# The sigmoid-gated activation of a fused attention/MLP/MoE kernel: ScalarE's Sigmoid with VectorE's product, against ScalarE's Gelu_apprx_sigmoid evaluated twice from PSUM

## Chip, cores, metric

The kernel runs on one core of one Trainium2 chip, as one launch. The metric is the device time of that launch in microseconds, the median of several runs. Engines are named as in the profile: PE is TensorE (PEld its weight loads), DVE is VectorE, ACT is ScalarE, POOL is GpSimd, SP is SyncE, whose queue starts most DMAs.

## What is computed

Three stages on 4608 tokens of width 512: a linear attention, an MLP with a sigmoid-gated activation, and a mixture of eight experts. The change is in the activation `g` of the MLP:

```python
def _attn_ref(q, k, v):                 # 8 batches, 8 heads, 576 x 64
    q_s = softmax(q, axis=-1)           # over the head's width
    k_s = softmax(k, axis=2)            # over the sequence
    kv = np.einsum('bhsd,bhse->bhde', k_s, v)
    return np.einsum('bhsd,bhde->bhse', q_s, kv)

def _moe_ref(x, w_in, w_out):           # 512 -> 2048 -> 512
    h = x @ w_in
    g = h * (1.0 / (1.0 + np.exp(-1.702 * h)))
    return g @ w_out

def _moe2_ref(x, w_skip, w_gate, w1, w2):   # E = 8 experts, 512 -> 1024 -> 512
    # tokens with x @ w_skip > 0 go to the expert of the largest gate logit
    h = np.maximum(xc[mask] @ w1[e], 0.0)
    y[mask] = gate_w[mask, None] * (h @ w2[e])
    out[do_compute] = xc + y
```

The inputs are float32, the MLP's weights float64. Matmuls keep float32 accuracy by splitting each operand into an upper half (rounded to fp32r) and the rest (lower half): three fp32r matmuls, upper by upper, upper by lower and lower by upper, stand for one.

## The kernel before

The tokens are worked in nine chunks of 512 (`NCH`). For each chunk the MLP runs over 16 blocks m of 128 hidden units. `mm1(m)` (L441 to L443) makes the block's `h` in a PSUM bank `hps[m % 2]` out of 12 matmuls; `mm1_act(m)` turns it into `ghi[m % 3]` (upper half) and `glo[m % 3]` (lower half) in SBUF; `mm2(m)` (L470 to L472) multiplies these with `w_out` into four accumulators in 12 matmuls. The activation has four steps: `act_sig` (ACT, L446) writes sigmoid(1.702 h) into the one tile `sgt`; `act_mul` (DVE, L449) multiplies it with `h` out of the bank, in place; `act_hi` (ACT, L452) rounds `sgt` into `ghi`; `act_lo` (DVE, in the first and the last chunk POOL, L455) subtracts `ghi` from `sgt` into `glo`. The bank is free for block m+2 when `act_mul` has read it, and `sgt` is free for block m+1 when `act_lo` has read it.

Every engine works off its own instructions in the order in which the code issues them.

- **The start (chunk 0)** is issued in the order of the words of the string `START`: `sg`, `sm`, `gh` and `gl` with a block's number are the four steps above. Between them stand the attention of chunks 0 and 1 (`ka` is L269, DVE's maximum over K; `kb` L275 and `kt` L266 are PE transposes; `kv` L301 the product of K and V) and the splitting of the MLP's weights, piece by piece: `wl` loads 128 x 512 float64 (SP), `wa` takes the absolute value into one of two temporaries (ACT, L197), `wb` makes a float32 out of the bits in four steps on DVE (L209 to L212), `wh` rounds the upper half (ACT, L221), `wp` subtracts for the lower half (POOL, L225).
- **Chunks 1 to 8** run the loop over m: `mm1(m + 2)`, its `mm1_act`, `mm2(m)`, and then what the list `slots[m]` holds: attention for the next chunk, the gate's dot products of the chunk before (L487, DVE), and its routing. `route_b` (L569, L570) puts counts into a PSUM tile `att`, of which there are two; `route_c` (L577 to L592) is a chain of small DVE instructions that reads it. After m = 14 and 15 the next chunk's input is made by `x_prod` (L408, PE, into `att`) and split (L393 ACT, L420 DVE). `exp` of the attention and of the routing needs another ACT function table than the activation does, so an ACT_TABLE_LOAD stands at each switch.
- **The experts** follow the last chunk; there the activation is Relu (L973), which the change doesn't touch.

Of the kernel before, what the change touches and what calls it, by code (L numbers as in the profile page):

```python
# [40 lines left out]
START = """  # L41
kl.0.1 ql.0.0 ql.0.1 kl.0.0 kl.0.2 km.0.1 kl.0.3 kt.0.1 vl.0.1 ka.0.1 qm.0.0 kb.0.1 vl.0.3 ks.0.1
qs.0.0:G qm.0.1 ke.0.1 vl.0.0 km.0.0 qs.0.1:G qe.0.0 qr.0.0 wl.0.0.0 kt.0.0 vl.0.2 qe.0.1 km.0.2
qn.0.0:G kv.0.1 km.0.3 wl.5.1.1 qt.0.0.1 wl.1.0.2 ka.0.0 wl.0.2.3 qt.0.0.0 kb.0.0 qc.0.0.1:A qr.0.1
wl.0.1.6 qc.0.0.0:A wl.0.3.7 ks.0.0 wl.1.1.8 wl.4.1.9 wa.0.0.0 ke.0.0 kt.0.2 qn.0.1:G kr.0.1
wl.1.3.10 kn.0.1:V ka.0.2 wl.4.3.11 kt.0.3 kb.0.2 ka.0.3 qt.0.1.1 wl.4.0.12 ks.0.2 kb.0.3 qc.0.1.1:A
wl.1.2.13 ks.0.3 qt.0.1.0 ql.1.0 xm.0.1 ke.0.3 kv.0.0 wb.0.0 ct xh.0.1:A ke.0.2 cw wa.0.2.0 kr.0.0
vl.1.0 xl.0.1 kn.0.0:A kv.0.3 wb.0.2 qc.0.1.0:A kv.0.2 kl.1.1 wh.0.0 kr.0.3 vl.1.1 kr.0.2 wp.0.0:G
kn.0.3:A kn.0.2:V xm.0.3 wa.0.1.0 wb.0.1 ql.1.1 xm.0.2 xh.0.3:A wl.5.0.0 xl.0.3 xh.0.2:A kl.1.0
wh.0.1 xl.0.2 wa.4.1.0 wp.0.1:G xm.0.0 wl.4.2.5 xh.0.0:A wb.4.1 wl.5.2.4 wl.2.0.6 wh.0.2 wh.4.1  # L50
xl.0.0 m1.0 wp.0.2:G wa.1.1.0 wb.1.1 wl.2.1.3 m1.1 sg.0 wp.4.1:G sm.0 wa.4.0.0 wb.4.0 wh.1.1
wl.2.3.9 gh.0 gl.0:G m1.2 wa.0.3.1 wh.4.0 qm.1.0 wb.0.3 wa.1.0.0 sg.1 c2t c2c wp.4.0:G wh.0.3 c2d
sm.1 gh.1 m2.0 wb.1.0 wa.1.3.1 wl.5.3.12 wb.1.3 wa.1.2.0 wh.1.0 wb.1.2 wp.0.3:G gl.1:G wl.2.2.7 m1.3
sg.2 wh.1.3 wa.4.2.1 m2.1 wh.1.2 wb.4.2 wp.1.1:G wp.1.0:G wl.6.2.2 wa.5.0.0 wh.4.2 wp.1.3:G sm.2
wa.4.3.1 qm.1.1 gh.2 wp.1.2:G gl.2:G km.1.1 m1.4 km.1.0 wp.4.2:G sg.3 sm.3 wb.4.3 wl.3.0.5 m2.2 gh.3
wb.5.0 qs.1.0:G qe.1.0 m1.5 wa.2.1.1 wh.4.3 gl.3:G wh.5.0 qr.1.0 wa.2.0.0 kt.1.0 sg.4 wp.4.3:G
ka.1.0 sm.4 kt.1.1 kb.1.0 wp.5.0:G gh.4 m2.3 ka.1.1 gl.4:G m2.4 ks.1.0 wl.6.0.0 ke.1.0 wb.2.1 sg.5
kl.1.2 sm.5 wa.2.2.1 wb.2.2 qn.1.0:G gh.5 kb.1.1 m1.6 wh.2.1 wh.2.2 wb.2.0 qs.1.1:G wa.5.2.1 kv.1.0
m1.7 wb.5.2 gl.5:G wp.2.1:G wl.6.1.3 sg.6 vl.1.2 wh.2.0 wa.5.1.0 wb.5.1 wp.2.2:G wh.5.2 wa.2.3.1
wh.5.1 wb.2.3 wp.2.0:G wa.6.1.0 wp.5.1:G sm.6 qe.1.1 wa.5.3.1 kr.1.0 gh.6 wb.5.3 wl.7.2.1 wh.2.3  # L60
m2.5 kn.1.0:A wp.2.3:G wa.6.0.1 qr.1.1 wh.5.3 gl.6:G m1.8 km.1.2 wp.5.2:G sg.7 sm.7 wp.5.3:G m2.6
wl.3.1.4 gh.7 ks.1.1 wb.6.0 ke.1.1 kl.1.3 kt.1.2 m1.9 ka.1.2 gl.7:G wh.6.0 wa.3.0.1 wp.6.0:G sg.8
sm.8 m2.7 wl.3.2.0 wb.3.0 gh.8 gl.8:G m1.10 km.1.3 wa.3.1.1 wh.3.0 kt.1.3 wp.3.0:G sg.9 m2.8 sm.9
gh.9 wb.6.1 wl.3.3.5 wh.6.1 wb.3.1 wa.3.2.0 m1.11 wb.3.2 gl.9:G sg.10 wa.6.2.1 kb.1.2 wh.3.1 wb.6.2
wp.6.1:G wl.6.3.3 m2.9 wa.3.3.0 wh.3.2 wh.6.2 wb.3.3 wp.3.1:G wl.7.1.4 wa.6.3.1 sm.10 wp.3.2:G
wh.3.3 wa.7.2.0 wp.3.3:G ka.1.3 kb.1.3 wl.7.3.0 gh.10 gl.10:G ks.1.2 kv.1.1 ks.1.3 m1.12 wl.7.0.5
kr.1.1 ke.1.2 vl.1.3 wb.6.3 kn.1.1:A sg.11 kv.1.2 wh.6.3 wp.6.2:G qt.1.0.0 sm.11 gh.11 wa.7.0.1
m1.13 kr.1.2 wb.7.2 ke.1.3 wh.7.2 wb.7.0 wa.7.1.0 m2.10 kn.1.2:A kv.1.3 wb.7.1 wp.6.3:G gl.11:G
sg.12 wh.7.0 m2.11 wa.7.3.1 wp.7.0:G sm.12 wh.7.1 gh.12 wp.7.1:G kr.1.3 kn.1.3:V m1.14 gl.12:G
qc.1.0.0:A m2.12 wb.7.3 sg.13 sm.13 wp.7.2:G qt.1.0.1 gh.13 gl.13:G m1.15 qc.1.0.1:A qn.1.1:V  # L70
qt.1.1.0 wh.7.3 sg.14 qt.1.1.1 wp.7.3:G sm.14 qc.1.1.0:A m2.13 qc.1.1.1:V c2b gh.14 gl.14:G sg.15
xm.1.3 m2.14 sm.15 xh.1.3:A xl.1.3 gh.15 gl.15:G xm.1.1 m2.15 xh.1.1:A xl.1.1 xm.1.0 xm.1.2 xh.1.0:A
xl.1.0 xh.1.2:A xl.1.2
"""
# [1247 lines left out]
```

## Time and profile before

| | us |
|---|---|
| median of 3 runs | 1301.46 |
| lowest and highest | 1297.41, 1302.84 |
| the profiled execution, its own time | 1297.15 |
| its span, first to last instruction | 1295.4 |
| chunk 0 (the start) in it | 0 to 186.7 |
| chunks 1 to 8 | 186.7 to 982.7 |
| experts | 982.7 to 1295.4 |

A row of the profile names line, engine, operation and tiles (out<-in). "Idle" is time in which the engine of the row had nothing to do, and behind the arrow stands the instruction that ended it. The granted clock of PE is given as a share of full speed, with 0.974 in the mean over the span. In the timeline a row has the start and the duration; instructions of one engine overlap by about 0.1 us, so the distance between two starts is shorter than the duration.

### The profile page before, as it was taken

What the parts mean: (1) busy time and instruction counts of PE and PEld (TensorE: products, weight loads), DVE (VectorE), ACT (ScalarE), POOL (GpSimd) and SP (SyncE); (2) the same over time, 40 slices, a digit from 0 to 9 for tenths busy, and PEclk for the clock granted to TensorE, in tenths of its full rate; (3) what the DMA queues carried; (4) which work ended last, traced back from release to release, by engine and by line L of the source; (5) the groups of instructions that cost most, each with busy time, mean ns of one, the idle gap of its engine ahead of it and who ended that gap; (6) DMA issues with size and microseconds to landing.
All of it is one profiled execution on the core that took longest, in us unless ns stands there. A gap on an engine that the chain in (4) does not pass through costs nothing. (4 is left out here: it accounts for less than half of the span.)

```text
span 1295.4 us, 17224 instructions
## 1 busy us (share of the span) xinstructions
PE 1214.2 (94%) x6316; PEld 990.4 (76%) x6316; DVE 907.6 (70%) x1791; ACT 571.3 (44%) x774; POOL 204.0 (16%) x185
## 2 busy tenths in 40 slices
...
GB/s 288 238 52 74 91 168 67 47 25 92 50 6 114 48 11 107 46 19 99 47 27 98 37 1 98 1 1 66 27 234 99 169 280 209 256 215 233 222 168 142
DMA packets 109857, 138.25 MB, mean 107 GB/s; under 512 B 52805, under 2 KB 72517, under 8 KB 107314
## 3 DMA queue, kind: packets, MB, share of 16 engines
...
q14 instruction: 55, 0.45, 0.1%
...
## 5 line engine op out<-in xcount | busy, mean ns | idle before, releaser
L441 PE MATMUL hps<-xth,wh 128*128 128x512 f32 x576 | 238.4, 414 | 10.6 <-ACT wh L221 8.9
L470 PE MATMUL acc<-wh,ghi 128*128 128x512 f32 x576 | 232.2, 403 | 9.2 <-ACT wh L221 9.2
L442 PE MATMUL hps<-xtl,wh 128*128 128x512 f32 x576 | 229.9, 399 | 0.9 <-DVE xtl L420 0.9
L443 PE MATMUL hps<-xth,wl 128*128 128x512 f32 x576 | 229.9, 399 | 0.7 <-POOL wl L225 0.7
L471 PE MATMUL acc<-wl,ghi 128*128 128x512 f32 x576 | 227.8, 396 | 1.6 <-POOL wl L225 1.6
L472 PE MATMUL acc<-wh,glo 128*128 128x512 f32 x576 | 228.1, 396 | 0.5 <-POOL glo L455 0.5
L449 DVE TENSOR_TENSOR sgt<-hps,sgt 128x512 f32<-128x512 f32 x144 | 99.4, 690 | 157.6 <-ACT sgt L446 156.9
L446 ACT ACTIVATE sgt<-hps 128x512 f32<-128x512 f32 x144 | 86.2, 598 | 200.3 <-PE hps L443 174.5
L487 DVE CUSTOM_DVE_ANT_0 qb<-qx,wgb 128x512 f32<-128x512 f32 x225 | 160.6, 714 | 3.2
...
L452 ACT CAST ghi<-sgt 128x512 fp32r<-128x512 f32 x144 | 89.3, 620 | 127.8 <-DVE sgt L449 125.5
L441 PEld LDWEIGHTS hps<-xth,wh 128*128 128x128 f32 x576 | 111.1, 193 | 39.7 <-ACT wh L221 9.8
L470 PEld LDWEIGHTS acc<-wh,ghi 128*128 128x128 f32 x576 | 109.2, 190 | 35.0 <-ACT wh L221 9.6
L443 PEld LDWEIGHTS hps<-xth,wl 128*128 128x128 f32 x576 | 109.9, 191 | 27.6 <-POOL wl L225 1.1
L471 PEld LDWEIGHTS acc<-wl,ghi 128*128 128x128 f32 x576 | 109.1, 189 | 28.2 <-POOL wl L225 2.7
L442 PEld LDWEIGHTS hps<-xtl,wh 128*128 128x128 f32 x576 | 110.4, 192 | 24.5 <-DVE xtl L420 1.7
L472 PEld LDWEIGHTS acc<-wh,glo 128*128 128x128 f32 x576 | 109.2, 190 | 25.9 <-POOL glo L455 1.0
L966 PE MATMUL hps<-ghi,wh 128*128 128x256 f32 x352 | 100.3, 285 | 0.1
L968 PE MATMUL hps<-ghi,wl 128*128 128x256 f32 x352 | 99.1, 281 | 0.0
L967 PE MATMUL hps<-glo,wh 128*128 128x256 f32 x352 | 99.0, 281 | 0.0
L455 DVE TENSOR_TENSOR glo<-sgt,ghi 128x512 fp32r<-128x512 f32 x112 | 77.6, 693 | 26.0 <-ACT ghi L452 19.3
L983 PE MATMUL acc<-wh,xth 128*128 128x512 f32 x192 | 77.0, 401 | 0.0
...
## 6 DMA issues: line engine op xcount, KB each, us to landing
...
```

The costliest lines, as they stand in the source:

```text
L441: nc.tensor.matmul(hp, lhsT=wh[s][:, kk, cs], rhs=xth[:, kk], start=(kk == 0), stop=False)
L442: nc.tensor.matmul(hp, lhsT=wh[s][:, kk, cs], rhs=xtl[:, kk], start=False, stop=False)
L443: nc.tensor.matmul(hp, lhsT=wl[s][:, kk, cs], rhs=xth[:, kk], start=False, stop=(kk == 3))
L449: nc.vector.tensor_mul(out=sgt, in0=hps[m % 2], in1=sgt)
L452: nc.scalar.copy(out=ghi[m % 3], in_=sgt)
L470: nc.tensor.matmul(acc[r], lhsT=gh[:, cs], rhs=wh[4 + s][:, mm], start=(m == 0), stop=False)
L471: nc.tensor.matmul(acc[r], lhsT=gh[:, cs], rhs=wl[4 + s][:, mm], start=False, stop=False)
L472: nc.tensor.matmul(acc[r], lhsT=gl[:, cs], rhs=wh[4 + s][:, mm], start=False, stop=(m == 15))
L487: nc.vector.tensor_tensor_reduce(out=out, in0=qx[:, r, :], in1=wgb[:, e, :], scale=1.0, scalar=0.0, op0=ALU.mult, op1=ALU.add, accum_out=l ...
L966: nc.tensor.matmul(o, lhsT=wh[w][:, kk, cs], rhs=xh, start=(kk == 0), stop=False)
L967: nc.tensor.matmul(o, lhsT=wh[w][:, kk, cs], rhs=xl, start=False, stop=False)
L968: nc.tensor.matmul(o, lhsT=wl[w][:, kk, cs], rhs=xh, start=False, stop=(kk == 3))
```

## The change

`act_sig` and `act_mul` go. `act_hi` now evaluates `Gelu_apprx_sigmoid` on the PSUM bank and writes the rounded result straight into `ghi`; the new `act_all` evaluates the same function on the same bank once more and writes it unrounded into `sgt`. Both are on ACT. `act_lo` stays. In `START` the word `gh` moves to the place of `sg`, the new word `ga` (`act_all`) stands where `gh` stood, and `sm` is gone; all other words keep their order.

```diff
 START = """
...
-xl.0.0 m1.0 wp.0.2:G wa.1.1.0 wb.1.1 wl.2.1.3 m1.1 sg.0 wp.4.1:G sm.0 wa.4.0.0 wb.4.0 wh.1.1
-wl.2.3.9 gh.0 gl.0:G m1.2 wa.0.3.1 wh.4.0 qm.1.0 wb.0.3 wa.1.0.0 sg.1 c2t c2c wp.4.0:G wh.0.3 c2d
-sm.1 gh.1 m2.0 wb.1.0 wa.1.3.1 wl.5.3.12 wb.1.3 wa.1.2.0 wh.1.0 wb.1.2 wp.0.3:G gl.1:G wl.2.2.7 m1.3
+wb.1.1 wl.2.1.3 m1.1 gh.0 wp.4.1:G wa.4.0.0 wb.4.0 wh.1.1 wl.2.3.9 ga.0 gl.0:G m1.2 wa.0.3.1 wh.4.0
+qm.1.0 wb.0.3 wa.1.0.0 gh.1 c2t c2c wp.4.0:G wh.0.3 c2d ga.1 m2.0 wb.1.0 wa.1.3.1 wl.5.3.12 wb.1.3
...
-    def act_sig(m):
-        nc.scalar.activation(out=sgt, in_=hps[m % 2], func=AF.Sigmoid, scale=1.702)
-
-    def act_mul(m):
-        nc.vector.tensor_mul(out=sgt, in0=hps[m % 2], in1=sgt)
-
     def act_hi(m):
-        nc.scalar.copy(out=ghi[m % 3], in_=sgt)
+        nc.scalar.activation(out=ghi[m % 3], in_=hps[m % 2], func=AF.Gelu_apprx_sigmoid)
+
+    def act_all(m):
+        nc.scalar.activation(out=sgt, in_=hps[m % 2], func=AF.Gelu_apprx_sigmoid)
...
     def mm1_act(m, eng=nc.vector, fill=()):
-        act_sig(m)
-        act_mul(m)
         act_hi(m)
+        act_all(m)
         for f in fill:
             f()
         act_lo(m, eng)
...
-        "sg": act_sig,
-        "sm": act_mul,
         "gh": act_hi,
+        "ga": act_all,
         "gl": act_lo,
```

The instructions of each engine, as they stand in the two programs (line numbers of the later one are a few lower; the number behind a tile's name is its buffer):

DVE in the start, around block 8, before. L209 to L212 are a piece of weights, L269 and L256 maxima over K:

```order
L212 SCALAR_TENSOR_TENSOR wgb<-wgb 128x512
L269 TENSOR_REDUCE kmx<-att 128x1
L449 TENSOR_TENSOR sgt<-hps,sgt 128x512
L209 TENSOR_SCALAR wgb<-wgb 128x512
L210 TENSOR_SCALAR wgb<-wgb 128x512
L211 SCALAR_TENSOR_TENSOR wgb<-qx,wgb 128x512
L212 SCALAR_TENSOR_TENSOR qx<-qx,wgb 128x512
L256 TENSOR_REDUCE kpm_98<-kvr 128x128
L449 TENSOR_TENSOR sgt<-hps,sgt 128x512
L209 TENSOR_SCALAR kvr<-kvr 128x512
```

The same place after:

```order
L211 SCALAR_TENSOR_TENSOR wgb<-wgb 128x512
L268 TENSOR_REDUCE kmx<-att 128x1
L208 TENSOR_SCALAR wgb<-wgb 128x512
L209 TENSOR_SCALAR wgb<-wgb 128x512
L210 SCALAR_TENSOR_TENSOR wgb<-qx,wgb 128x512
L211 SCALAR_TENSOR_TENSOR qx<-qx,wgb 128x512
L255 TENSOR_REDUCE kpm_98<-kvr 128x128
L208 TENSOR_SCALAR kvr<-kvr 128x512
```

The two products are gone from between the pieces, and nothing else has moved.

DVE at the end of chunk 1, block 15 and the beginning of `route_c`, before:

```order
L550 TENSOR_TENSOR roh<-roh,rcm 128x32
L552 TENSOR_SCALAR rval<-misc 128x4
L449 TENSOR_TENSOR sgt<-hps,sgt 128x512
L455 TENSOR_TENSOR glo_89<-sgt,ghi_86 128x512
L577 COPY rrk<-att 128x32
```

After:

```order
L545 TENSOR_TENSOR roh<-roh,rcm 128x32
L547 TENSOR_SCALAR rval<-misc 128x4
L451 TENSOR_TENSOR glo_89<-sgt,ghi_86 128x512
L572 COPY rrk<-att 128x32
L574 TENSOR_TENSOR rrk<-rrk,misc 128x8
```

The subtraction is now the block's only instruction on DVE, ahead of `route_c`.

ACT at the same place, before:

```order
L558 ACT_TABLE_LOAD
L558 ACTIVATE rex<-rex 128x32
L446 ACT_TABLE_LOAD
L446 ACTIVATE sgt<-hps 128x512
L452 CAST ghi_86<-sgt 128x512
L393 COPY qx<-att 128x512
```

After:

```order
L553 ACT_TABLE_LOAD
L553 ACTIVATE rex<-rex 128x32
L445 ACT_TABLE_LOAD
L445 ACTIVATE ghi_86<-hps 128x512
L448 ACTIVATE sgt<-hps 128x512
L392 COPY qx<-att 128x512
```

ACT has as many instructions as before, in the same places, with as many table loads; the second of the block reads PSUM and no longer what DVE wrote.

## Rows read from the trace of the kernel before

**Rows 1.** Page, part 1: busy time and instructions of each engine.

```profile
PE 1214.2 (94%) x6316; PEld 990.4 (76%) x6316; DVE 907.6 (70%) x1791; ACT 571.3 (44%) x774; POOL 204.0 (16%) x185
```

**Rows 2.** Windows: stretch, length; busy (instructions) of PE, PEld, DVE, ACT, POOL; PE's clock, DMA.

```profile
46.00:146.30 100.30, 65.87 (x265) 49.31 (x263) 93.19 (x116) 52.00 (x78) 47.30 (x34) 0.85 0.34 113
146.30:186.70 40.40, 39.93 (x215) 31.09 (x215) 25.24 (x40) 23.14 (x37) 17.79 (x13) 0.91 0.36 105
389.00:488.00 99.00, 97.74 (x500) 78.39 (x498) 70.83 (x166) 44.50 (x65) 2.93 (x3) 1.00 0.21 56
```

**Rows 3.** Waits of PE in the start (total, times, longest), and PE's timeline at 146.

```profile
PE att L275 <- DVE kmx L269: 12.1, 3, 8.1
PE acc L470 <- ACT wh L221: 9.2, 1, 9.2
...
146.32 0.47 PE L275 MATMUL att<-ident,kmx 128*128 128x128 f32 x1 [8.07 <-DVE kmx L269]
```

**Rows 4.** Groups of DVE by form, 46 to 146.3: count, busy, mean ns, idle before.

```profile
L211 DVE SCALAR_TENSOR_TENSOR wgb<-qx,wgb 128x512 uint32<-128x512 uint32 x4 | 7.1, 1775 | 0.1
L449 DVE TENSOR_TENSOR sgt<-hps,sgt 128x512 f32<-128x512 f32 x10 | 6.8, 684 | 4.3 <-ACT sgt L446 4.3
...
L212 DVE SCALAR_TENSOR_TENSOR qx<-qx,wgb 128x512 uint32<-128x512 uint32 x4 | 2.8, 693 | 0.2
```

**Rows 5.** Timeline of DVE in the start around blocks 5 and 8: start, duration.

```profile
89.53 0.70 DVE L212 SCALAR_TENSOR_TENSOR wgb<-wgb 128x512 uint32<-128x512 uint32 x1
90.14 0.68 DVE L449 TENSOR_TENSOR sgt<-hps,sgt 128x512 f32<-128x512 f32 x1
90.95 0.43 DVE L209 TENSOR_SCALAR wgb<-wgb 128x512 f32<-128x512 f32 x1
...
120.06 0.28 DVE L269 TENSOR_REDUCE kmx<-att 128x1 f32<-128x128 f32 x1
123.35 0.69 DVE L449 TENSOR_TENSOR sgt<-hps,sgt 128x512 f32<-128x512 f32 x1 [3.00 <-ACT sgt L446]
123.95 0.42 DVE L209 TENSOR_SCALAR wgb<-wgb 128x512 f32<-128x512 f32 x1
```

**Rows 6.** Timeline of ACT at the same two places.

```profile
90.26 0.67 ACT L197 ACTIVATE wgb<-ewh 128x512 f32<-128x512 f32 x1 [2.88 <-DVE wgb L212]
...
120.74 0.67 ACT L197 ACTIVATE wgb<-qx 128x512 f32<-128x512 f32 x1
```

**Rows 7.** Groups of ACT by form, whole span: count, busy, mean ns, idle before.

```profile
L452 ACT CAST ghi<-sgt 128x512 fp32r<-128x512 f32 x144 | 89.3, 620 | 127.8 <-DVE sgt L449 125.5 <-DVE misc L915 2.3
L446 ACT ACTIVATE sgt<-hps 128x512 f32<-128x512 f32 x144 | 86.2, 598 | 200.3 <-PE hps L443 174.5 <-POOL glo L455 23.6 <-DVE glo L455 1.7
...
L973 ACT ACTIVATE xth<-hps 128x512 fp32r<-128x512 f32 x44 | 26.4, 600 | 104.6 <-issue 56.8 <-PE hps L968 40.3 <-ACT wh L928 7.6
```

**Rows 8.** Timelines of ACT, DVE and PE at the end of chunk 1.

```profile
275.24 0.60 ACT L446 ACTIVATE sgt<-hps 128x512 f32<-128x512 f32 x1
276.60 0.62 ACT L452 CAST ghi<-sgt 128x512 fp32r<-128x512 f32 x1 [0.76 <-DVE sgt L449]
...
277.25 0.69 DVE L455 TENSOR_TENSOR glo<-sgt,ghi 128x512 fp32r<-128x512 f32 x1 [0.68 <-ACT ghi L452]
277.86 0.19 DVE L577 COPY rrk<-att 128x32 f32<-128x32 f32 x1
...
277.01 0.39 PE L570 MATMUL att<-roh,ones 128*128 128x32 f32 x2
277.75 1.14 PE L408 MATMUL att<-qx,qb 128*128 128x128 f32 x4 [0.36 <-ACT qx L393]
279.77 0.46 PE L408 MATMUL att<-qx,qb 128*128 128x128 f32 x2 [0.88 <-DVE rrk L581]
```

**Rows 9.** Line 408 over the whole span: idle of PE before it, by releaser (us, times).

```profile
  DVE rrk L581: 6.2, 7
```

**Rows 10.** Timeline of PE at the end of the last chunk.

```profile
980.26 0.50 PE L472 MATMUL acc<-wh,glo 128*128 128x512 f32 x1 [0.52 <-POOL glo L455]
```

More of the change, by code (lines that the diff above doesn't have):

```diff
@@ L44 @@
 qn.0.0:G kv.0.1 km.0.3 wl.5.1.1 qt.0.0.1 wl.1.0.2 ka.0.0 wl.0.2.3 qt.0.0.0 kb.0.0 qc.0.0.1:A qr.0.1
[L45 to L49, printed above, removed]
@@ L50 @@
-wh.0.1 xl.0.2 wa.4.1.0 wp.0.1:G xm.0.0 wl.4.2.5 xh.0.0:A wb.4.1 wl.5.2.4 wl.2.0.6 wh.0.2 wh.4.1
-xl.0.0 m1.0 wp.0.2:G wa.1.1.0 wb.1.1 wl.2.1.3 m1.1 sg.0 wp.4.1:G sm.0 wa.4.0.0 wb.4.0 wh.1.1
-wl.2.3.9 gh.0 gl.0:G m1.2 wa.0.3.1 wh.4.0 qm.1.0 wb.0.3 wa.1.0.0 sg.1 c2t c2c wp.4.0:G wh.0.3 c2d
-sm.1 gh.1 m2.0 wb.1.0 wa.1.3.1 wl.5.3.12 wb.1.3 wa.1.2.0 wh.1.0 wb.1.2 wp.0.3:G gl.1:G wl.2.2.7 m1.3
-sg.2 wh.1.3 wa.4.2.1 m2.1 wh.1.2 wb.4.2 wp.1.1:G wp.1.0:G wl.6.2.2 wa.5.0.0 wh.4.2 wp.1.3:G sm.2
-wa.4.3.1 qm.1.1 gh.2 wp.1.2:G gl.2:G km.1.1 m1.4 km.1.0 wp.4.2:G sg.3 sm.3 wb.4.3 wl.3.0.5 m2.2 gh.3
@@ L56 @@
[L56 to L73, printed above, removed]
+wl.0.1.6 qc.0.0.0:A wl.0.3.7 ks.0.0 wl.1.1.8 wl.4.1.9 wa.0.0.0 ke.0.0 kt.0.2 qn.0.1:G kr.0.1 wl.1.3.10
@@ new lines @@
+kn.0.1:V ka.0.2 wl.4.3.11 kt.0.3 kb.0.2 ka.0.3 qt.0.1.1 wl.4.0.12 ks.0.2 kb.0.3 qc.0.1.1:A wl.1.2.13
+ks.0.3 qt.0.1.0 ql.1.0 xm.0.1 ke.0.3 kv.0.0 wb.0.0 ct xh.0.1:A ke.0.2 cw wa.0.2.0 kr.0.0 vl.1.0 xl.0.1
+kn.0.0:A kv.0.3 wb.0.2 qc.0.1.0:A kv.0.2 kl.1.1 wh.0.0 kr.0.3 vl.1.1 kr.0.2 wp.0.0:G kn.0.3:A kn.0.2:V
+xm.0.3 wa.0.1.0 wb.0.1 ql.1.1 xm.0.2 xh.0.3:A wl.5.0.0 xl.0.3 xh.0.2:A kl.1.0 wh.0.1 xl.0.2 wa.4.1.0
+wp.0.1:G xm.0.0 wl.4.2.5 xh.0.0:A wb.4.1 wl.5.2.4 wl.2.0.6 wh.0.2 wh.4.1 xl.0.0 m1.0 wp.0.2:G wa.1.1.0
@@ new lines @@
+wb.1.1 wl.2.1.3 m1.1 gh.0 wp.4.1:G wa.4.0.0 wb.4.0 wh.1.1 wl.2.3.9 ga.0 gl.0:G m1.2 wa.0.3.1 wh.4.0
+qm.1.0 wb.0.3 wa.1.0.0 gh.1 c2t c2c wp.4.0:G wh.0.3 c2d ga.1 m2.0 wb.1.0 wa.1.3.1 wl.5.3.12 wb.1.3
+wa.1.2.0 wh.1.0 wb.1.2 wp.0.3:G gl.1:G wl.2.2.7 m1.3 gh.2 wh.1.3 wa.4.2.1 m2.1 wh.1.2 wb.4.2 wp.1.1:G
+wp.1.0:G wl.6.2.2 wa.5.0.0 wh.4.2 wp.1.3:G wa.4.3.1 qm.1.1 ga.2 wp.1.2:G gl.2:G km.1.1 m1.4 km.1.0
+wp.4.2:G gh.3 wb.4.3 wl.3.0.5 m2.2 ga.3 wb.5.0 qs.1.0:G qe.1.0 m1.5 wa.2.1.1 wh.4.3 gl.3:G wh.5.0 qr.1.0
@@ new lines @@
+wa.2.0.0 kt.1.0 gh.4 wp.4.3:G ka.1.0 kt.1.1 kb.1.0 wp.5.0:G ga.4 m2.3 ka.1.1 gl.4:G m2.4 ks.1.0 wl.6.0.0
+ke.1.0 wb.2.1 gh.5 kl.1.2 wa.2.2.1 wb.2.2 qn.1.0:G ga.5 kb.1.1 m1.6 wh.2.1 wh.2.2 wb.2.0 qs.1.1:G
+wa.5.2.1 kv.1.0 m1.7 wb.5.2 gl.5:G wp.2.1:G wl.6.1.3 gh.6 vl.1.2 wh.2.0 wa.5.1.0 wb.5.1 wp.2.2:G wh.5.2
+wa.2.3.1 wh.5.1 wb.2.3 wp.2.0:G wa.6.1.0 wp.5.1:G qe.1.1 wa.5.3.1 kr.1.0 ga.6 wb.5.3 wl.7.2.1 wh.2.3
+m2.5 kn.1.0:A wp.2.3:G wa.6.0.1 qr.1.1 wh.5.3 gl.6:G m1.8 km.1.2 wp.5.2:G gh.7 wp.5.3:G m2.6 wl.3.1.4
```

11 lines of the change are left out of this document (added).

## The prediction

> **What bounds the kernel now.** I read the busy times first. PE is busy for 1214.2 of 1295.4 us and ACT for 571.3, DVE for 907.6 [rows 1]. So the product that goes, an instruction of DVE, counts only where PE waits for DVE. The windows tell where that can be. In a middle chunk PE is busy for 97.74 of 99.00 us at full clock [rows 2]: no more than 1.26 us a chunk are to be had there. Between 46 and 146.3 us, in the start, it is the other way round: PE is busy for 65.87 of 100.30 us, and DVE for 93.19 [rows 2]. The waits of PE in the start agree: it waits for DVE's maximum over K, or for weights that ACT rounds and that DVE has made just before; the longest such wait ends at 146.32, after 8.07 us, by a DVE instruction [rows 3]. From there to the end of the start PE is busy for 39.93 of 40.40 us [rows 2]. So the start is a queue of DVE up to 146 us and a queue of PE behind it: what DVE wins before 146, PE gets as a whole, and what it wins later is worth nothing.
>
> **The change part by part.**
>
> *The product in the start.* Ten of the 144 products lie between 46 and 146.3, with 684 ns each and 4.3 us of idle time before three of them [rows 4]. The next instruction starts about 0.61 us after a product does (123.95 is 0.60 after 123.35 [rows 5]). So at most 10 x 0.61 = 6.1 us and the 4.3 us of waiting come out: 10.4 us. Not all of it does:
> - Block 5, at 90.14: the next piece needs ACT's absolute value, which begins at 90.26, when DVE has left the temporary, and takes 0.67; so L209 can't start before 90.95 with or without the product [rows 5, 6]. This product covers a wait of ACT. Block 6, at 107.43, stands in the same way. Minus 2 x 0.61 = 1.2.
> - Block 8: DVE is free at 120.34, waits 3.00 us for the sigmoid, and then multiplies. The piece behind it had its input at 120.74 + 0.67 = 121.41 [rows 5, 6]. So 1.1 of the 3.00 us stay as a wait for ACT; 123.95 becomes 121.45.
> - Block 4: its idle time goes, but the next subtraction waits for a transpose of PE; I take 0.3 off.
>
> 10.4 - 1.2 - 1.1 - 0.3 = **7.8 us**. Bounds: 10.4 above, and below about 2 (the first rival).
>
> *What takes its place on ACT.* The upper half's rounding of 620 ns (sgt to ghi) becomes an evaluation from PSUM into fp32r, and the sigmoid becomes a second evaluation from PSUM into f32. No row shows this function. The nearest are the Sigmoid, 598 ns from PSUM to f32, and the Relu, 600 ns from PSUM to fp32r [rows 7]. At 600 each ACT has 1200 instead of 1218 ns a block: nothing. I take 600; how long it would have to be to hurt is the second rival. [...]
>
> *The wait that is added.* PE's `mm1(m + 2)` needs the bank, and now waits for ACT's second evaluation instead of DVE's product. That evaluation stands where the rounding stood, which began right behind the product: the bank comes free up to 0.66 us later where ACT is late. In the loop 12 matmuls of `mm2` and more lie between; in the start PE has 100.30 - 65.87 = 34.4 us of idle time in the stretch [rows 2]. Nothing, and without this cover 0.66 a block. The other wait gets better: `act_hi` no longer waits for `act_lo` of the block before (23.6 us of ACT waiting for POOL in all [rows 7]); only `act_all` does.
>
> *The end of each chunk.* PE's L408 waits 0.36 us for a copy of ACT and then 0.88 for DVE's `route_c` [rows 8]; the second happens 7 times, 6.2 us in all [rows 9]. `route_c` (L577 at 277.86) follows the subtraction L455 at 277.25, which waits for sigmoid, product and rounding in turn: 2.01 us from 275.24 [rows 8]. Now the two evaluations follow each other on ACT, about 0.5 us apart (0.60 less the overlap), and end at 276.35; the subtraction starts at 276.38 and has passed on DVE by 276.99. But `route_c` also needs PE's L570, whose modelled end is 277.01 + 0.39 = 277.40. It starts at about 277.43, 0.43 earlier, and so does PE. 7 x 0.43 = **3.0 us**. Bounds: 0, if PE's end is later than modelled, and 7 x (0.36 + 0.88) = 8.7, if both waits go.
>
> *The last chunk.* POOL makes the lower half there, and PE waits for it once, 0.52 us [rows 10]. The last product stood behind DVE's splitting of expert weights; the evaluation doesn't. **0.5 us**, bound 0.
>
> *Blocks 11 to 15 of the start and the other products of the loop* lie where PE is busy: nothing. The experts are untouched; they begin earlier.
>
> Sum: 7.8 + 3.0 + 0.5 = 11.3 us. Against the profiled execution's own 1297.15 us this is 1285.9. That execution lay 4.3 us under the median, 1301.46, so the median should be 1290.2.
>
> **The rivals.**
>
> *The start gives part of it back.* DVE and POOL hinder each other here: the same kind of weight step takes 693 ns (L212) when it is alone and 1775 (L211) where POOL is subtracting [rows 4], 1.08 more. POOL is busy for 47.30 us of the stretch [rows 2]. The product is not among the struck ones, at 684 in the mean [rows 4]; so it is a stretch in which POOL may run at no cost, and without it POOL's work falls on weight steps. Each further struck step gives back 1.08. Five of them: 11.3 - 5.4 = 5.9, 1295.6; all ten: 0.5, 1301. For it: POOL's instruction follows the rounding of a piece and so falls into the next piece anyway. Against: only two of the ten products had POOL beside them, at 70.25 and 129.11, and what triggers POOL moves along with DVE. [...]
>
> *Slower: the function takes longer than the Sigmoid.* Place: the 20 evaluations in the DVE stretch, if DVE's pieces wait for ACT's absolute values behind them, and the two before each `route_c`. If each takes T, the chunk's end loses when 2T - 0.06 is over 2.01, T over 1.04; the start loses when 20 x (T - 0.60) is over 7.8, T over 0.99, with all of it on the path. So it decides from about 1.0 us. At twice the time, 1.2, the start gives 12.0 - 7.8 = 4.2 more and the chunk ends 7 x 0.33 = 2.3: 1308. Against it: Sigmoid and Relu, two functions that share nothing, differ by 2 ns [rows 7].
>
> *More than forecast.* The whole 10.4 in the start and both waits of each chunk's end: 10.4 + 8.7 + 0.5 = 19.6, 1282. It needs pieces on ACT to move up too, since ACT's rounding no longer waits for DVE (125.5 us of idle time in all [rows 7]), and L570 to end sooner than modelled.
>
> *That the change doesn't do what it says* could only be a table load more; the order has as many, at the same places.
>
> **How the numbers follow.** Forecast (1286 to 1294) 0.63; part given back (1294 to 1301) 0.20; more than forecast (1280 to 1286) 0.12; slower function (over 1304) 0.05. The likeliest time is 1290. For 8 in 10 the range leaves out the slow function, the worst quarter of the given-back case and the end of the largest gain: 1283 to 1298. A measurement tells about 0.5% from no change, 6.5 us, so faster is below 1295: the forecast with nine in ten of its chance (0.58), all of the larger gain (0.12) and a small share of the given-back case (0.03), 0.73; same 0.21; slower 0.06, the slow function and a little for what I haven't seen.
>
> **What would show it.** In the changed profile chunk 0 ends near 179 instead of 186.7, with PE's last long wait for the maximum over K ending near 138.5; the second wait before L408 is about 0.45 instead of 0.88, and the first stays near 0.3; both evaluations take about 600 ns; DVE is 144 x 0.69 = 99 us less busy and the middle chunks' PE is as dense as before. The prediction is wrong if weight steps of over 1.6 us become more frequent, if chunk 0 ends after 183, if an evaluation takes over 0.8 us, or if PE starts to wait for `sgt` or `ghi` in the loop.

## The result, and the profile after

The changed kernel takes 1286.63 us in the median of seven runs (1285.38 to 1292.31), the kernel before 1299.61 us beside it (seven runs, 1297.37 to 1302.84): a ratio of 0.9909, with an interval of 0.9886 to 0.9932. In a second comparison it was 1287.73 against 1299.24, 0.9907 (0.9888 to 0.9925). The forecast was 1290, in a range of 1283 to 1298. The profiled executions lie 11.3 us apart in their spans, 1295.4 and 1284.1.

Part 1 of the page of the changed kernel, busy time and instructions of each engine, answers to [rows 1]:

```profile
PE 1212.7 (94%) x6316; PEld 989.9 (77%) x6316; DVE 822.0 (64%) x1647; ACT 554.4 (43%) x774; POOL 203.1 (16%) x185
```

VectorE has the 144 products less, ScalarE as many instructions as before. That 85.6 us of VectorE's work bring 11.3 shows how much of it lay beside TensorE. ScalarE's groups by form (count, busy and mean ns, idle before), against [rows 7]:

```profile
L445 ACT ACTIVATE ghi<-hps 128x512 fp32r<-128x512 f32 x144 | 86.2, 598 | 262.7 <-PE hps L442 262.3
L448 ACT ACTIVATE sgt<-hps 128x512 f32<-128x512 f32 x144 | 85.4, 593 | 2.5 <-POOL glo L451 2.5
```

Both evaluations cost what the Sigmoid cost. The upper half now waits for TensorE alone; the 125.5 us of waiting for VectorE are gone, and of the 23.6 for GpSimd 2.5 are left, at L448. The windows, over the same stretches as [rows 2] and one of a middle chunk (stretch, length; busy and instructions of PE, PEld, DVE, ACT, POOL; PE's clock, DMA):

```profile
46.00:146.30 100.30, 71.08 (x297) 53.90 (x296) 93.53 (x113) 56.93 (x86) 52.18 (x36) 0.83 0.37 120
146.30:186.70 40.40, 40.21 (x212) 31.48 (x211) 20.25 (x31) 20.15 (x35) 14.06 (x10) 0.99 0.37 125
379.00:478.00 99.00, 98.17 (x500) 78.61 (x499) 63.04 (x152) 43.23 (x67) 2.92 (x3) 1.00 0.21 56
```

VectorE is as busy in the start as before, 93.53 against 93.19 us: it is still the engine that sets the pace there, and it gets to the end of its queue earlier. Two of TensorE's waits from 0 to 180 us (total, times, longest), and the end of the last long one in the timeline (start, duration), against [rows 3]:

```profile
PE hps L440 <- ACT sgt L448: 10.2, 2, 9.6
PE att L274 <- DVE kmx L268: 9.5, 3, 6.6
...
139.70 0.48 PE L274 MATMUL att<-ident,kmx 128*128 128x128 f32 x1 [6.63 <-DVE kmx L268]
```

146.32 has become 139.70. The first row is the wait that the prediction added, TensorE's for the bank until the second evaluation. But its longest case, which ends at 67.86, is not new: at the same place the kernel before waited for weights that ScalarE rounds.

```profile
66.96 0.76 PE L441 MATMUL hps<-xth,wh 128*128 128x512 f32 x1 [8.91 <-ACT wh L221]
```

So the second evaluation makes TensorE start 0.90 us later there (67.86 against 66.96). It lies beside VectorE's queue, which waits for TensorE only once, 0.22 us. VectorE around blocks 5 and 8, against [rows 5]:

```profile
89.34 0.43 DVE L208 TENSOR_SCALAR wgb<-wgb 128x512 f32<-128x512 f32 x1 [0.74 <-ACT wgb L196]
...
118.61 1.13 DVE L208 TENSOR_SCALAR wgb<-wgb 128x512 f32<-128x512 f32 x1 [1.08 <-ACT wgb L196]
```

Where the two products stood, VectorE now waits for ScalarE's absolute value: 0.74 us, and 1.08 of the former 3.00. The end of chunk 1, where [rows 8] has the same of before (timelines of ACT, DVE and PE):

```profile
268.04 0.60 ACT L445 ACTIVATE ghi<-hps 128x512 fp32r<-128x512 f32 x1
268.53 0.59 ACT L448 ACTIVATE sgt<-hps 128x512 f32<-128x512 f32 x1
269.16 0.69 DVE L451 TENSOR_TENSOR glo<-sgt,ghi 128x512 fp32r<-128x512 f32 x1 [3.18 <-ACT sgt L448]
...
270.47 0.39 PE L565 MATMUL att<-roh,ones 128*128 128x32 f32 x2
270.90 0.19 DVE L572 COPY rrk<-att 128x32 f32<-128x32 f32 x1 [1.05 <-PE att L565]
271.17 1.14 PE L407 MATMUL att<-qx,qb 128*128 128x128 f32 x4 [0.31 <-ACT qx L392]
...
272.83 1.11 PE L407 MATMUL att<-qx,qb 128*128 128x128 f32 x4 [0.53 <-DVE rrk L576]
```

`route_c` now begins 0.43 us after L565 does (270.90, 270.47), before 0.85 after L570 (277.86, 277.01). It no longer follows the subtraction, it waits for TensorE. The two waits of L407 are 0.31 and 0.53 instead of 0.36 and 0.88.

### The profile page after: what moved, and what is told of

It is laid out like the page before. It is cut to its first block, busy times and chain, and to the rows that moved or that the text cites. A ratio compares the mean times of both kernels' runs of the same rounds, so it can differ in the third digit from the quotient of the medians.

```text
span 1284.1 us, 16956 instructions
## 1 busy us (share of the span) xinstructions
PE 1212.7 (94%) x6316; PEld 989.9 (77%) x6316; DVE 822.0 (64%) x1647; ACT 554.4 (43%) x774; POOL 203.1 (16%) x185
## 4 chain that ended last, share of the span: by engine, by line
PE 82%; DVE 8%; DMA 4%; issue 4%; SPq 1%; POOL 0%; ACT 0%; POOLq 0%; DVEq 0%
PE hps L440 10%; PE acc L465 10%; PE acc L467 10%; PE hps L442 10%; PE hps L441 10%; PE acc L466 10%; PE hps L960 3%; PE hps L962 3%; PE hps L961 3%; PE acc L977 3%; PE acc L978 3%; PE acc L979 3%; DMA out_dram<-qx,misc 2%; PE att L300 2%; PE att L407 2%
## 5 line engine op out<-in xcount | busy, mean ns | idle before, releaser
L445 ACT ACTIVATE ghi<-hps 128x512 fp32r<-128x512 f32 x144 | 86.2, 598 | 262.7 <-PE hps L442 262.3
L467 PEld LDWEIGHTS acc<-wh,glo 128*128 128x128 f32 x576 | 109.1, 189 | 25.0
L448 ACT ACTIVATE sgt<-hps 128x512 f32<-128x512 f32 x144 | 85.4, 593 | 2.5 <-POOL glo L451 2.5
L923 DVE TENSOR_TENSOR wl<-wgb,wh 128x2048 fp32r<-128x2048 f32 x26 | 59.6, 2292 | 28.7 <-ACT wh L922 28.7
```

Of the source, the lines that this page charges most:

```text
L445: nc.scalar.activation(out=ghi[m % 3], in_=hps[m % 2], func=AF.Gelu_apprx_sigmoid)
L467: nc.tensor.matmul(acc[r], lhsT=gl[:, cs], rhs=wh[4 + s][:, mm], start=False, stop=(m == 15))
```

## Where the time goes, stage by stage

The table cuts each profiled execution at three rows of its timeline: the start of VectorE's last subtraction for the input of chunk 0 (L420 of before), the first `x_prod` at the end of chunk 0 (L408), and the end of the last evacuation of chunk 8. "VectorE's queue" is the part of the start from that subtraction to VectorE's last maximum over K (L269).

| kernel | up to the subtraction | start | of it VectorE's queue | loop | rest | span |
|---|---|---|---|---|---|---|
| before | 36.6 | 140.1 | 109.4 | 806.8 | 311.9 | 1295.4 |
| after | 36.6 | 133.5 | 102.7 | 803.1 | 310.9 | 1284.1 |
| after, again | 37.7 | 133.4 | 103.1 | 803.1 | 311.8 | 1286.0 |
| start only | 39.4 | 133.6 | 103.3 | 807.2 | 315.4 | 1295.6 |
| loop only | 38.4 | 140.5 | 109.7 | 803.1 | 314.6 | 1296.6 |
| idle instruction, waiting | 39.0 | 140.2 | 109.1 | 805.4 | 320.5 | 1305.1 |
| idle instruction, no wait | 36.6 | 136.3 | 105.4 | 805.3 | 312.7 | 1290.9 |
| each evaluation twice | 39.2 | 136.7 | 104.2 | 804.8 | 318.7 | 1299.5 |
| lower half on VectorE | 36.9 | 130.1 | 97.9 | 803.1 | 313.3 | 1283.4 |
| evaluated once | 39.3 | 133.4 | 103.5 | 803.1 | 317.4 | 1293.2 |
| one more tile | 37.2 | 133.2 | 102.4 | 805.3 | 311.7 | 1287.4 |
| late route | 38.1 | 133.5 | 103.1 | 808.9 | 314.3 | 1294.7 |
| late route, not in chunk 7 | 37.8 | 133.5 | 103.1 | 796.0 | 309.8 | 1277.1 |
| the same, absolute value first | 37.2 | 132.0 | 101.6 | 796.0 | 310.4 | 1275.6 |

The first column (loads) and the rest (the experts, the same in all) move by 2.8 and 10.7 us from one execution to the next, with no regard to the edit; start and loop repeat to a few tenths where the code is the same. So the experiments are read by stage, and a difference of a few us between medians isn't, unless a stage shows it.

## The experiments

**Each part alone.** The start only: the loop has sigmoid, product and rounding again.

```diff
     def mm1_act(m, eng=nc.vector, fill=()):
-        act_hi(m)
-        act_all(m)
+        nc.scalar.activation(out=sgt, in_=hps[m % 2], func=AF.Sigmoid, scale=1.702)
+        nc.vector.tensor_mul(out=sgt, in0=hps[m % 2], in1=sgt)
+        nc.scalar.copy(out=ghi[m % 3], in_=sgt)
```

> Chunk 0 has the two evaluations, the loop over chunks 1 to 8 keeps sigmoid, product and rounding. My theory (the start is a queue of VectorE, and the loop has only its chunk ends to give): chunk 0 ends near 180.1 as in the changed kernel, the two waits before x_prod are 0.36 and 0.88 us again, and the span is 1295.4 - 6.5 = 1288.9 us; should the 1.0 us that the experts won come from the start as well, 1287.9. Rival (the two parts depend on one another, because the loop starts with other buffers and clocks): the gain is clearly not 6.5 to 7.5 us, and this kernel and the loop-only one do not add up to 11.3.

The loop only is the kernel before with those lines exchanged the other way round:

> Chunk 0 keeps sigmoid, product and rounding, chunks 1 to 8 have the two evaluations. My theory: chunk 0 ends at 186.7, each of seven chunk ends is 0.43 us shorter (3.0), the last chunk 0.8, so the span is 1295.4 - 3.8 = 1291.6 us, or 1290.6 if the 1.0 us of the experts belong here. Rival (the loop wins nothing, the 2.9 us between the ends of chunk 0 and chunk 7 come from what the start shifted): 1295 us.

Measured: start only 1291.21 us, ratio 0.9940 (0.9923 to 0.9957); loop only 1297.12, 0.9977 (0.9961 to 0.9993). The spans expected, 1288.9 and 1291.6, were missed by 6.7 and 5.0, of which 6.3 and 4.5 lie in the first and the last column of the table. By stage the parts are additive: start only has the start of the changed kernel (133.6) and the loop of before (807.2), loop only the reverse (140.5 and 803.1). The start gives 6.8 us (140.3, the mean of two, against 133.5), the loop 3.9 (807.0, the mean of two, against 803.1). The expectation that the experts' 1.0 us belongs to one part has nothing for it: their stage is longer in both.

**What in the product cost the time: its duration, or its wait?** The changed kernel gets an instruction of VectorE in the old places, whose result nobody uses (additional work of 0.68 us):

```diff
+    fsc = sb("fsc", [P, 1])
...
+    def fill(m):
+        nc.vector.tensor_reduce(out=fsc, in_=hps[m % 2], op=ALU.max, axis=AX)
...
+        "sm": fill,
```

> The changed kernel, and in chunk 0 VectorE takes the maximum over the PSUM bank (128x512) where the product stood; nothing waits for its result, and it waits for no ScalarE step. It gives back VectorE's time alone and not the old chain sigmoid, product, rounding. My theory (the start won VectorE's time): ten such instructions of 0.6 us lie in the stretch, two of them where VectorE waits for ScalarE anyway, so 8 x 0.61 = 4.9 us come back less what the remaining wait of 1.1 us covers (one of 0.6): chunk 0 ends near 184.4 to 185, the span is 1288.4 to 1289. Rival (the start won by the shorter chain on ScalarE, and VectorE's time counts for little): chunk 0 ends near 180.5 and the span stays at 1284 to 1285. A second rival, by the strikes: if the instruction is a shelter for GpSimd's work as the product was, one or two struck weight steps go and the loss is 1 us smaller, 3.3 to 4.2.

Measured: 1299.26 us, ratio 1.0004 (0.9987 to 1.0021); a start of 140.2: the whole gain of it is gone, where 4.3 to 4.9 us of it were expected to go. The waits of VectorE in its queue tell why (total, times, longest):

```profile
DVE fsc L456 <- ACT ghi L447: 6.4, 4, 3.0
```

The instruction was meant to wait for no step of ScalarE. But reading the same bank it is placed behind the evaluation, and so it stands in for the product with its wait too. This run therefore shows something else than intended: an instruction of VectorE at this place, tied to ScalarE, costs the start 6.7 us, a maximum that nobody uses as much as the product. To part the two, it reads a tile in SBUF that is long complete:

```diff
-        nc.vector.tensor_reduce(out=fsc, in_=hps[m % 2], op=ALU.max, axis=AX)
+        nc.vector.tensor_reduce(out=fsc, in_=xth[:, 0].bitcast(F32), op=ALU.max, axis=AX)
```

> As the idle-product kernel, but VectorE's instruction (the maximum over 128x512) reads a tile in SBUF that is long complete, so it takes VectorE's time at the old place and waits for nobody; in the run before, it read the bank and was made to wait 6.4 us for ScalarE's evaluation, as the product was. My theory (the start won both: VectorE's time, and the waits behind ScalarE): of the 8.8 us between the two, the time alone is 8 x 0.61 = 4.9 us less 0.6 that a remaining wait covers: the last maximum over K is used at 4.3 us later than in the changed kernel beside it. Rival 1 (the wait on ScalarE was the whole cost): 0 to 1 us later. Rival 2 (the time is the whole cost, and the wait is only where it shows): 8 us or more later.

Measured: 1293.63 us (0.9971, 0.9947 to 0.9994), a start of 136.3. So of 6.7 us (140.2 less 133.5) the duration brings back 2.8 and the wait 3.9. My 4.3 was too high and both rivals were wrong. Eleven instructions take 7.4 us, of which less than half arrives, since VectorE waits less for ScalarE where they stand (2.9 us in its queue instead of 5.6), and its 93 weight steps are shorter (80.4 us instead of 81.8 in the changed kernel's second execution). At block 0, in two rows of VectorE's timeline, the piece behind the instruction still waits 1.73 us, against 1.77 and 2.46 in the two executions of the changed kernel:

```profile
41.26 0.68 DVE L456 TENSOR_REDUCE fsc<-xth 128x1 f32<-128x512 f32 x1
43.67 0.43 DVE L210 TENSOR_SCALAR kvr<-kvr 128x512 f32<-128x512 f32 x1 [1.73 <-ACT kvr L198]
```

**Evaluated once.** The first step writes sgt from PSUM, the second rounds it as before:

```diff
     def act_hi(m):
-        nc.scalar.activation(out=ghi[m % 3], in_=hps[m % 2], func=AF.Gelu_apprx_sigmoid)
+        nc.scalar.activation(out=sgt, in_=hps[m % 2], func=AF.Gelu_apprx_sigmoid)
     def act_all(m):
-        nc.scalar.activation(out=sgt, in_=hps[m % 2], func=AF.Gelu_apprx_sigmoid)
+        nc.scalar.copy(out=ghi[m % 3], in_=sgt)
```

> The changed kernel, but the function is evaluated once, from PSUM into sgt, and the second step is a rounding copy of sgt on ScalarE as before: VectorE's product is gone without the second evaluation. My theory (what counts is that VectorE's instruction and its wait are gone; the second evaluation only takes the place of the copy at the same duration): within 2 us of the changed kernel, stretch of VectorE in the start 103 us, chunks 101.0 us apart, second wait before x_prod 0.5 us. Rival (the direct evaluation into the upper half is worth something, since it needs no sgt and so doesn't wait for the subtraction of the block before): 2 to 6 us slower, with ScalarE's waits for GpSimd's lower half back.

Measured: 1292.15 us (0.9933, 0.9911 to 0.9956; four runs from 1288.37 to 1294.92). Start 133.4 and loop 803.1, those of the changed kernel: what counts is that VectorE is out of the chain, and the second evaluation is worth no more than the copy. The median is 4.4 us above the changed kernel's 1287.73, which was not taken beside it; the intervals of the two ratios overlap. In the profile the difference lies wholly in the first stage and in the experts. No stage that the edit touches explains it; whether it is chance over four runs stays open.

**Each evaluation twice**, to price the slower function:

```diff
     def act_hi(m):
-        nc.scalar.activation(out=ghi[m % 3], in_=hps[m % 2], func=AF.Gelu_apprx_sigmoid)
+        for _ in range(2):
+            nc.scalar.activation(out=ghi[m % 3], in_=hps[m % 2], func=AF.Gelu_apprx_sigmoid)
```

and the same in `act_all`.

> The changed kernel with each of the two evaluations done twice (the same result written again), so that the upper half is ready after 1.1 and everything after 2.2 us instead of 0.55 and 1.1. It prices the rival that the function takes longer than the Sigmoid. The prediction's bounds for twice the time: the start at most 12 us later (20 evaluations of 0.6 in the stretch, all of them on the path), each of seven chunk ends 0.76 us (2 x 1.2 - 0.06 - 1.57) and so 5.3, against the changed kernel. My theory: ScalarE is busy for only half of the start, so that a third of the 12 us or less arrives, 2 to 5 us, and the chunk ends give their 5.3 whole: 1291 to 1295. Rival (everything on the path): 1304 or more. Rival (all hidden): within 2 us of the changed kernel.

Measured: 1293.52 us (0.9945, 0.9929 to 0.9962), 5.8 over the changed kernel beside it, and still faster than before. The start is 3.2 us longer, not 12 (1.1 of it in VectorE's queue, 104.2 against 103.1), and the chunks are 101.12 us apart instead of 101.00 (mean distance of `x_prod` over five chunks); the loop takes 1.7 more. The chunk end of this kernel:

```profile
274.96 1.22 ACT L450 ACTIVATE sgt<-hps 128x512 f32<-128x512 f32 x2
...
276.21 0.69 DVE L453 TENSOR_TENSOR glo<-sgt,ghi 128x512 fp32r<-128x512 f32 x1 [3.17 <-ACT sgt L450]
...
278.74 1.11 PE L407 MATMUL att<-qx,qb 128*128 128x128 f32 x4 [0.64 <-DVE rrk L578]
```

With 1.2 us for each, the second wait of L407 is 0.64 us, well under the 0.88 of before. The prediction had it decide at 1.04 us.

**GpSimd's price.** The lower halves of blocks 0 to 10 of the start go to VectorE (in `START`, `gl.0:G` to `gl.10:G` become `gl.0:V` to `gl.10:V`):

> The changed kernel with the lower halves of blocks 0 to 10 of chunk 0 on VectorE instead of GpSimd. It prices the strikes: between the last subtraction of x and the last maximum over K, VectorE takes 103.1 us in the changed kernel (four executions: 102.7 to 103.3), of which 82.8 are its 92 weight steps, 27 of them over 1.2 us. My theory (each GpSimd subtraction that runs beside a weight step costs that step up to 1 us): eleven subtractions of 0.61 us come to VectorE, 6.7 us, and the weight steps get 5 to 8 us shorter as fewer are struck, so the stretch is 101 to 105 us long and the time within 2 us of the changed kernel. Rival (GpSimd's other subtractions, of the weights, strike the same steps anyway): the weight steps stay at 81 or more and the stretch grows to 108 us or more, 5 us slower.

Measured: 1285.27 us (0.9885, 0.9869 to 0.9902). VectorE's queue is 97.9 us long instead of 103.1, though ten subtractions were added to it: a larger gain than either theory had. (The eleventh, of block 10, stands behind the last maximum over K in `START` and so behind the queue.) The windows of the weight steps alone, lines 209, 210 and 211 over that queue, show why (stretch, length, busy and count; then clock and DMA). The changed kernel, second execution:

```profile
37.72:140.77 103.05, 15.35 (x23) 0.85 0.39 123
37.72:140.77 103.05, 29.11 (x23) 0.85 0.39 123
37.72:140.77 103.05, 23.27 (x24) 0.85 0.39 123
```

With the lower halves on VectorE:

```profile
36.93:134.82 97.89, 10.81 (x23) 0.86 0.41 130
36.93:134.82 97.89, 23.59 (x23) 0.86 0.41 130
36.93:134.82 97.89, 20.71 (x24) 0.86 0.41 130
```

That is 12.6 us less in the three lines, and 13.3 with line 208 (14.06 to 13.39). So each of the ten subtractions on GpSimd had made VectorE's weight steps 1.3 us longer in the mean, and on VectorE itself it takes 0.85 (8.53 us for the ten). 1.9 of the 5.2 us are lost again behind the queue: from the last maximum to `x_prod` it is 32.2 us instead of 30.3. TensorE is not busy for longer there (29.09 us against 29.32); it waits. Two rows of this run, and TensorE's of the changed kernel:

```profile
136.66 0.84 DVE L451 TENSOR_TENSOR glo<-sgt,ghi 128x512 fp32r<-128x512 f32 x1 [1.56 <-ACT sgt L448]
...
138.29 1.55 PE L300 MATMUL att<-kvr 128*64 128x65 f32 x20 [2.81 <-DVE kvr L283]
```

```profile
141.84 1.54 PE L300 MATMUL att<-kvr 128*64 128x65 f32 x20 [0.25 <-DVE kvr L283]
```

The eleventh subtraction waits on VectorE for ScalarE's second evaluation, and the subtraction of the maximum (L283), for which TensorE waits, stands behind it. So the start wins 3.3 us. Leaving block 10 on GpSimd wasn't tried.

**The waits at the chunk ends.** `x_prod` takes its PSUM tiles right behind `route_b`'s and the last transposes'. The late route takes `route_b` away from there:

```diff
-                at(13, route_b)
-                at(13, route_c)
-                at(13, route_gate)
+                at(15, route_b)
+                at(15, route_c)
+                at(15, route_gate)
                 for r in range(4):
-                    at(14 + r // 2, route_d, r)
+                    at(15, route_d, r)
```

> The changed kernel with route_b, route_c, route_gate and route_d of chunks 1 to 7 behind block 15 instead of block 13, so that x_prod no longer takes its PSUM tiles right behind route_b's. My theory (the two waits before x_prod, 0.31 and 0.53 us, are waits for the two buffers of that tile and nothing else): both go, 7 x 0.84 = 5.9 us, span 1278.2. If only the second goes: 7 x 0.53 = 3.7, 1280.4. Rival (the wait moves: TensorE now waits for route_b's own buffer or for an evacuation behind route_c on VectorE at the chunk's boundary): 1284 or up to 7 x 2 us slower, 1298.

Measured: 1297.16 us (0.9980, 0.9964 to 0.9997), slower than the changed kernel. But the chunks are 99.82 us apart, 1.18 less: both waits are gone, and 0.34 more; `x_prod`, no longer broken up by them, takes 1.97 us for its eight matmuls (L407 at 271.80) instead of 1.14 and 1.11. The loss is one wait in chunk 8. GpSimd's timeline there:

```profile
886.81 1.18 POOL L591 DMA_INDIRECT table<-rval,rpi  x1 [3.10 <-DMA table<-rval,rpi]
894.12 1.32 POOL L591 DMA_INDIRECT table<-rval,rpi  x1 [6.13 <-DMA table<-rval,rpi]
895.45 1.28 POOL L451 TENSOR_TENSOR glo<-sgt,ghi 128x512 fp32r<-128x512 f32 x1
...
896.78 0.80 PE L467 MATMUL acc<-wh,glo 128*128 128x512 f32 x1 [12.24 <-POOL glo L451]
```

The writes of the routing in chunk 7 wait for one another, each for the landing of the one ahead; the lower halves of chunk 8 are queued behind them. The changed kernel has the same queue, but its four writes begin 3.1 us into chunk 8 (first `x_prod` to first write, second execution); here they begin 13.0 us into it. So chunk 7 keeps its routing at block 13 (`rs = 13 if j == NCH - 2 else 15`):

> As the late-route kernel, but chunk 7 keeps its routing at block 13. In the late-route kernel chunks 1 to 6 became 1.3 to 1.6 us shorter each than in the changed kernel, and chunk 8 lost 12.2 us in one wait of TensorE for GpSimd's lower half, since GpSimd's queue held the last routing's writes ahead of it. My theory: chunks 1 to 6 keep their gain, 6 x 1.4 = 8.4 us, chunk 7 and 8 are as in the changed kernel, so it is 8 us faster than the changed kernel beside it. Rival (the late writes of the routing delay the lists at the end of chunk 7 as well): chunk 8 loses 5 us or more again.

Measured: **1281.75 us** (0.9874, 0.9845 to 0.9904), 6.0 under the changed kernel beside it, 7.1 by the loop.

**The queue of ScalarE at block 0.** Three rows of the changed kernel's second execution show what the prediction had not looked at: the first evaluation stands at the head of ScalarE's queue, waits for its bank, and the absolute value for which VectorE waits stands behind it.

```profile
43.35 0.60 ACT L445 ACTIVATE ghi<-hps 128x512 fp32r<-128x512 f32 x1 [2.99 <-PE hps L442]
43.84 0.66 ACT L196 ACTIVATE kvr<-ewl 128x512 f32<-128x512 f32 x1
...
44.53 0.43 DVE L208 TENSOR_SCALAR kvr<-kvr 128x512 f32<-128x512 f32 x1 [2.46 <-ACT kvr L196]
```

On top of the late route, the two change places:

```diff
-m1.1 gh.0 wp.4.1:G wa.4.0.0 wb.4.0
+m1.1 wp.4.1:G wa.4.0.0 gh.0 wb.4.0
```

> The late-route kernel of 1281.75 us (chunks 1 to 6 late, chunk 7 as it was), and in chunk 0 the first evaluation gh.0 stands behind wa.4.0.0 and no longer ahead of it. In the changed kernel ScalarE waits 2.99 us for block 0's bank at the head of its queue, and behind it stands the absolute value for which VectorE waits 2.46 us. My theory: VectorE gets its piece 1.7 us earlier (it has left the temporary at 42.0, 0.67 us for the absolute value), the stretch of the start becomes 101.3 us instead of 103.1, and the time about 1280. Rival (the gain is given back by strikes or by another wait for ScalarE): 103 us and 1281.7.

Measured: **1280.91 us** (0.9857, 0.9841 to 0.9874), the lowest median of all. VectorE's row of the same place is now

```profile
42.62 0.43 DVE L208 TENSOR_SCALAR kvr<-kvr 128x512 f32<-128x512 f32 x1 [0.72 <-ACT kvr L196]
```

1.7 us less of waiting, and 1.5 us less in the start (133.5 to 132.0). The lower halves on VectorE weren't tried together with these two.

**The changed kernel again, and one more tile.**

> The changed kernel once more, on the chip and in the hour of the other runs, to see how far the stages of one and the same program move between executions. So far the start ended at 180 us with these instructions in one execution and about 3 us later in another (start only), and the experts, which no kernel here touches, took from 307.9 to 317.4 us from the last evacuation to the end, with 3.1 to 8.6 us of TensorE waiting for the gather of the tokens. My theory: chunk 0 ends between 180 and 184, the chunks are 101.0 us apart as before, the experts differ by the wait for the gather alone, and the median is 9 to 13 us under the kernel before. Rival (the 13 us of the first timing were a lucky placement): the median is within 6.5 us of the kernel before.

Measured: 1287.73 us, as told; start and loop repeat to 0.1 us. The tile of the idle-instruction kernels by itself (`fsc = sb("fsc", [P, 1])`, used by nothing):

> The changed kernel with one more tile of 128x1 in SBUF that nothing uses. In the two idle-product kernels, which have this tile, the chunks of the loop were 101.27 us apart instead of 101.0 with the same waits, since the matmuls in the second part of each chunk followed each other at 0.2325 us instead of 0.2285. Theory (the place of the tiles in SBUF, which the new tile shifts, sets it): 101.27 here too, 1.9 us slower than the changed kernel over the loop. Rival (it came from the additional instructions of those kernels, by another place of the program): 101.0 us, the same time.

Measured: 1292.89 us (0.9953, 0.9936 to 0.9970). The chunks are 101.28 us apart instead of 101.00, as in the two kernels that had the tile, and the loop is 2.2 us longer. So their longer loop came from the tile and not from the instruction; the theory holds that far. That it is the place of the tiles in SBUF, as the theory has it, is not shown.

## Why the prediction was right, step by step

**The bound.** VectorE's queue up to the last maximum over K, then TensorE's: right. Start and loop could be taken apart, and what VectorE won in its queue (6.7 us) arrived at `x_prod` (6.6). It needn't: of the 5.2 us that the lower halves on VectorE won there, 1.9 were lost behind it.

**The product in the start, 7.8 us.** The mechanism held, the size was 6.6 between the two profiles. Blocks 5, 6 and 8 came out as worked out (waits of 0.74, 0.62 and 1.08 us), and block 4 too (0.22 for the 0.3 taken). The term that was short is the first rival, in small. The 93 weight steps of the queue took 80.3 us before (lines 209 to 212: 14.23 + 14.38 + 28.01 + 23.72) and 82.2 after (14.42 + 15.36 + 29.11 + 23.28): 1.8 us more on balance, worth not quite two strikes, where the forecast had none and the rival five. Some steps got longer and others shorter. The steps of over 1.6 us, a sign that the prediction named against itself, are 20 before and 20 after. 0.9 comes back where a step of the softmax takes 0.37 us (L369, at 110.31) instead of 1.28 (L370, at 112.88). The price of a strike, 1.08, was near: 1.3 us for each subtraction by the run with the lower halves on VectorE. Block 0, which lies ahead of the window from which the ten products were counted, comes out even: a product of 0.61 us and its wait of 1.07 went, a wait of 1.77 for an absolute value behind the first evaluation came (2.46 in the second execution).

**ScalarE: nothing.** Right: 598 and 593 ns against the 600 taken. The bound behind it was too strict. At twice the time the kernel was to take 1308; with both evaluations doubled it took 1293.52, 5.8 us more and not 18 (1308 less 1290). Most of that miss lies in the start, 3.2 us instead of 12: the bound put all 20 evaluations on the path. VectorE's waits for ScalarE grew by 3.2 us (5.6 to 8.8) and its weight steps got 2.7 shorter; how much of the 12 ScalarE's own idle time took up wasn't separated. The other step that failed is the chain at the chunk end, counted from the sigmoid at 275.24. In the trace of before the table load ahead of it waited for TensorE's bank:

```profile
273.95 1.28 ACT L446 ACT_TABLE_LOAD   x1 [0.69 <-PE hps L443]
```

All loads of this line together show the same (count, busy, mean ns, idle before), first before, then after:

```profile
L446 ACT ACT_TABLE_LOAD x41 | 52.6, 1283 | 23.9 <-PE hps L443 23.8
...
L445 ACT ACT_TABLE_LOAD x40 | 51.3, 1283 | 0.7
```

After, the load at the chunk end doesn't wait: it follows the `exp` of the routing at once, at 266.74, and is over at 268.02. Why it waits in the one kernel and not in the other isn't shown. The subtraction therefore starts 1.31 us ahead of L565 (269.16, 270.47); before, it started 0.24 behind L570 (277.25, 277.01). The prediction had it move up by 0.87; it was 1.55. Since `route_c` waits for TensorE's matmul in any case, this showed only in the doubled run.

**The wait that is added.** Right for the loop, where TensorE waits for no evaluation. In the start the bank is ready 1.0 us later at the one place where TensorE waits long (67.81, the end of the evaluation, against 66.81, the end of the product), more than the 0.66 taken; TensorE starts 0.90 later and VectorE's queue covers it.

**The chunk ends, 3.0 us.** 0.88 to 0.53 and 0.36 to 0.31, 0.40 a chunk and 2.8 over seven; 0.42 by the distance of the chunks. The modelled end of the matmul was good to 0.04 us (270.47 + 0.39 = 270.86 for L565, and `route_c` at 270.90). The bound of 7 x 1.24 = 8.7, with both waits gone, was too low for that case: with the late route, other code, a chunk is 1.60 us shorter than before (101.42, 99.82). That is also more than the 1.26 us that the prediction took from TensorE's busy time as all that a chunk could give; `x_prod` in one go got shorter in its busy time as well.

**The last chunk, 0.5 us.** It gave 0.8. From the first `x_prod` of chunk 7's end to the last evacuation it is 101.9 us before and 100.7 after; 0.35 of the difference is the shorter second wait, which is counted above. Of the rest TensorE's wait of 0.52 is gone, and the other 0.3 I couldn't place.

**The experts, 0.** They took 1.0 us less, and the sum, 1285.9, met the profiled execution's own time, 1285.86, to a tenth. That is chance: the start gave 1.2 us too little, the chunks a little more than forecast, and a stage that moves by up to 10.7 us between executions gave 1.0.

**The median.** The prediction added 4.3 us for the distance between the profiled execution and the median of three, 1301.46. Over seven runs the median of before was 1299.61, 2.5 above that execution, and the changed kernel's profile lay 0.8 under its own median. So the offset was in good part scatter, and it is the term that was too large in the forecast: with 0.8 in place of 4.3 the sum gives 1286.7, against the measured 1286.63.

**The signs.** VectorE is 85.6 us less busy and not 99: instructions of one engine overlap by about 0.1 us (0.11 for the two evaluations at 268.04 and 268.53), so a product adds some 0.6 us to the busy time, 144 x 0.6 = 86. The other signs came as told: 139.70 for 138.5, evaluations of 598 and 593 ns, and no wait of TensorE for `sgt` or `ghi` in the loop.
